# One PSUM tile of three banks becomes three tiles, and one copy of 1024 columns becomes two of 512

## The chip, the cores and the metric

The kernel runs on one core of a Trainium2 chip. The core has a tensor engine (PE), a vector engine (DVE), a scalar engine (ACT), GpSimd (POOL) and a sync engine (SP); here SP and POOL only issue DMAs once the start is over. The metric is the device time of one execution in microseconds (us). Lower is better.

## The reference

```python
def _attn_ref(q, k, v, tau):
    qn = q / (np.linalg.norm(q, axis=1, keepdims=True) + 1e-06)
    kn = k / (np.linalg.norm(k, axis=1, keepdims=True) + 1e-06)
    s = kn.transpose(0, 2, 1) @ qn / tau
    s = s - s.max(-1, keepdims=True)
    a = np.exp(s)
    a /= a.sum(-1, keepdims=True) + 1e-09
    return v @ a
...
def _moe_ref(x, w_in, w_out):
    h = x @ w_in
    g = h * (1.0 / (1.0 + np.exp(-h)))
    return g @ w_out
```

q, k and v are 2 x 6016 x 256 in float32. Attention is over the 256 channels, so each batch has one 256 x 256 matrix `a`. Its output, 12032 tokens of 256, goes through a feed-forward net of 2048 hidden channels: `w_in` (256 x 2048), SiLU, `w_out` (2048 x 256).

## The kernel before, in words

The kernel never forms `v @ a`. It multiplies `a` into `w_in` first (`mix`) and runs V, transposed, through the mixed weights. All large products run in float16, each operand as a high and a low half, three matmuls for each product (low x high, high x low, high x high). The first layer's 2 x 2 block products are computed with 7 block products in place of 8 (a Strassen-like scheme): sums of weight blocks S1 to S4 and of V blocks T1 to T4 are made ahead, and seven products are accumulated into three PSUM banks called z, y and x.

Tokens are worked in 12 pairs of up to 1024 columns, 6 to a batch; the last pair of a batch has 896. Pairs 0 and 5 are built by `emit_pair_group`, whose instructions a scheduler orders by priority and readiness. The other ten pairs are built by `emit_unit`, 8 units to a pair, and there PE, DVE and ACT keep the order in which the code is written. A unit works on two weight groups of 128 channels and on half of the pair's columns (256, or 224 in the last pair), so that a product is 6 matmuls of 256 columns that fill one bank of 512.

A unit goes like this. The products y (S1, L737) and x (A11, L738) are made, then one ACT copy moves both banks into `c51` (L740, 1024 columns). The product z (A12, L741) follows. `tail(0)` runs what earlier units left for this place. DVE subtracts z from the copied x (L743, helper L720). The products y (S4) and x (S2) are added into the banks (L745, L746), ACT copies x into `c2` (L748), DVE subtracts y from it (L751). The product x (S3, L753) follows, DVE subtracts the copied y from x (L754), the product x (A22, L758) follows. ACT applies SiLU to the four blocks (L723) and casts the top pair of them to float16 halves (L729, "high"); DVE makes the remainders (L732, "rest").

The second layer is spread over the next units. `out_of_unit` puts work into `later` lists: the remainder of the top pair, a sum of blocks that POOL makes by two DMAs (L902, L903, the second adding) and the cast of the low pair run in the next unit's `tail(0)`; the remainder of the low pair and a DVE sum (L896) in `tail(1)`; further sums, two of them by POOL's DMAs (L914, L915), in `tail(2)`. The second layer's matmuls (L822) are queued in groups of 4 and let out in blocks after each part of a unit: 8 matmuls after z, 12 after x (S2), 16 after x (S3), 8 after x (A22). After every fourth unit ACT copies four output banks (`take`, L866) and DVE joins them (L881, L885). In the gaps between the parts stand steps of background work: casts of the next pair's V (`scale_v`, ACT L164 and DVE L165), square sums of the transposed q and k in pairs 1 to 3, mixing for batch 1 in pairs 4 to 6.

The tile framework makes the semaphore waits. It follows every tile's readers and writers, so which tile a bank belongs to decides which waits it puts in.

Of the kernel before, what the change touches and what calls it, by code (L numbers as in the profile page):

```python
# [9 lines left out]
F32 = mybir.dt.float32  # L10
# [8 lines left out]
P = 128  # L19
# [11 lines left out]
def channel_attention_then_silu_ffn(ctx, tc, kq, qT, kT, vT, tau, w_in, w_out, outT):  # L31
    nc = tc.nc
# [12 lines left out]
    hp = ctx.enter_context(tc.tile_pool(name="hp", bufs=1))  # L45
    sm = ctx.enter_context(tc.tile_pool(name="sm", bufs=2))
    ps_b = ctx.enter_context(tc.tile_pool(name="ps_b", bufs=1, space=PSUM))
    zyx = ps_b.tile([P, 3, 512], F32, tag="zyx", name="zyx")
    z, y, x = (zyx[:, i] for i in range(3))
    ps_o = ctx.enter_context(tc.tile_pool(name="ps_o", bufs=4, space=PSUM))  # L50

    ident = const.tile([P, P], F32, name="ident")
# [29 lines left out]
    def room(name, n=1):  # L82

        k = turns[name] + turns[name] % n
        size = rooms[name].shape[1]
        k %= size
        turns[name] = (k + n) % size
        return rooms[name][:, k] if n == 1 else rooms[name][:, k : k + n]
# [611 lines left out]
    def emit_unit(p, u):  # L700


        b, n, w = pairs[p]
        h = w // 2
        m, alpha, sg = parts[p]
        which = 2 * (u % 4), 2 * (u % 4) + 1
        wide = h // 2
        at = u // 4 * wide

        def product(bank, a, x, first=False):  # L710
            for k, i in enumerate(which):
                for j, (v, c) in enumerate(((1, 0), (0, 1), (0, 0))):
                    nc.tensor.matmul(  # L713
                        bank[:, k * wide : (k + 1) * wide], mixed[b, i][:, v, a - 1],
                        m[:, c, x, at : at + wide], start=(first and j + k == 0),
                        stop=(j == 2), skip_group_check=True,
                    )

        def minus(g, a, c):
            nc.vector.tensor_tensor(out=g, in0=a[:, :h], in1=c[:, :h], op=ALU.subtract)  # L720

        def silu(src, g):
            nc.scalar.activation(out=g, in_=src, func=AF.Silu, scale=alpha)  # L723

        top, low = room("g", 2)[:, :, :h], room("g", 2)[:, :, :h]
        tops, lows = room("hl", 2)[:, :, :, :h], room("hl", 2)[:, :, :, :h]

        def high(hl, g):
            nc.scalar.activation(out=hl[:, :, 0], in_=g, func=AF.Copy, scale=sg)  # L729

        def rest(hl, g):
            nc.vector.scalar_tensor_tensor(  # L732
                out=hl[:, :, 1], in0=g, scalar=sg, in1=hl[:, :, 0], op0=ALU.mult,
                op1=ALU.subtract,
            )

        product(y, S1, T1, True)  # L737
        product(x, A11, B11, True)  # L738
        c51 = hp.tile([P, 2, 512], F32, tag="c51", name="c51")
        nc.scalar.copy(c51[:, :, :h], zyx[:, 1:, :h])  # L740
        product(z, A12, B21, True)  # L741
        tail(0)
        minus(top[:, 0], c51[:, 1], z)  # L743
        yield
        product(y, S4, B22)  # L745
        product(x, S2, T2)  # L746
        c2 = hp.tile([P, 512], F32, tag="c2", name="c2")
        nc.scalar.copy(c2[:, :h], x[:, :h])  # L748
        silu(top[:, 0], top[:, 0])
        tail(1)  # L750
        minus(top[:, 1], c2, y)  # L751
        yield
        product(x, S3, T3)  # L753
        minus(low[:, 1], x, c51[:, 0])  # L754
        silu(top[:, 1], top[:, 1])
        tail(2)
        yield
        product(x, A22, T4)  # L758
        silu(low[:, 1], low[:, 1])
        silu(x[:, :h], low[:, 0])  # L760
        high(tops, top)
        tail(3)
        out_of_unit(
            p, u, [tops[:, 0], tops[:, 1], lows[:, 0], lows[:, 1]], lambda: rest(tops, top),
            lambda: high(lows, low), lambda: rest(lows, low),
        )
        yield
# [4 lines left out]
    def tail(slot):  # L772

        for run in tails.pop(ticks[0], ()):
            run()
        ticks[0] += 1
# [555 lines left out]
```

## Time and profile before

| | |
|---|---|
| time, three runs | 1235.13, 1236.08 (median), 1240.56 us |
| the profiled execution | 1235.12 us, its span 1233.4 us |
| PE busy | 1065.3 us, 86% |
| DVE busy | 837.3 us, 68% |
| ACT busy | 815.0 us, 66% |
| POOL busy | 213.4 us, 17% |
| mean clock granted to PE | 0.988 of full speed |

The busy time of an engine is the time in which the profiler shows an instruction on it. Matmuls are pipelined and their ends are modelled, so consecutive matmuls overlap in the rows. An idle time is put down to the instruction that ended it, by semaphore events. The span is the profiled time of the program; the execution's own time is 1.7 us longer.

### The profile page before, as it was taken

The numbers are of one execution on the slowest core, as the hardware profiler recorded it, in microseconds if no ns is written. First come the engines' busy times: TensorE is split into PE (matmuls) and PEld (weight loads), VectorE is DVE, ScalarE is ACT, GpSimd is POOL, SyncE is SP. The second block draws the span as 40 slices with busy tenths as digits, with TensorE's granted clock in tenths as the row PEclk, the third lists the DMA queues.
The fourth block names the chain that finished last, engine by engine and source line by source line (L and its number), as shares of the span: only waits on it lengthen the run. The fifth ranks groups of instructions, "written<-read, shape, count | busy, mean of one in ns | idle before, by whom it ended". The sixth has DMA issues, their size and how long they took to land. (4 is left out here: it accounts for less than half of the span.)

```text
span 1233.4 us, 20497 instructions
## 1 busy us (share of the span) xinstructions
PE 1065.3 (86%) x8222; PEld 840.0 (68%) x8222; DVE 837.3 (68%) x1358; ACT 815.0 (66%) x1161; POOL 213.4 (17%) x301
## 2 busy tenths in 40 slices
PE   9999987887887887888999888888888888888886
PEld 8865534776766776766655677777777777777886
DVE  6895574675775666767778667767767767767665
ACT  6686666667675766666778566666666666666664
POOL 1010000211212121212100112212212212122232
PEclk9999998999998999999999999999999999999999
DMA  9982102544535535334200335335335335334444
GB/s 374 396 295 94 35 1 94 128 143 113 164 94 174 154 78 156 87 78 128 61 1 23 89 74 139 94 76 142 91 77 144 89 77 141 87 77 112 96 91 83
DMA packets 63793, 143.35 MB, mean 116 GB/s; under 512 B 6930, under 2 KB 21218, under 8 KB 63698
## 3 DMA queue, kind: packets, MB, share of 16 engines
q0 software_dynamic: 32944, 72.57, 25.3%
q1 hardware_dynamic: 30466, 68.95, 15.9%
q8 instruction: 64, 1.05, 0.4%
q10 hardware_dynamic: 288, 0.52, 0.1%
q14 instruction: 31, 0.25, 0.1%
HBM read 57.67 MB, written 12.32 MB: 57 GB/s over the span
## 5 line engine op out<-in xcount | busy, mean ns | idle before, releaser
L713 PE MATMUL zyx<-m,wall 128*128 128x256 f16 (+1 forms) x3360 | 433.0, 273 | 143.6 <-ACT c L740 92.1
L713 PEld LDWEIGHTS <-wall 128*128 128x128 f16 x3360 | 329.0, 98 | 228.9 <-issue 183.3
L732 DVE SCALAR_TENSOR_TENSOR hl<-g,sg,hl 128x1024 f16<-128x1024 f32 (+1 forms) x160 | 202.6, 1266 | 80.3 <-ACT hl L729 80.2
L822 PE MATMUL o<-hl,wo 128*128 128x256 f16 (+1 forms) x1920 | 240.9, 271 | 1.2 <-DVE hl L732 1.2
L822 PEld LDWEIGHTS <-wo 128*128 128x128 f16 x2240 | 218.9, 98 | 27.0 <-issue 2.2
L723 ACT ACTIVATE g<-g,alpha 128x512 f32<-128x512 f32 (+1 forms) x240 | 171.4, 715 | 53.9 <-DVE g L720 50.9
L729 ACT ACTIVATE hl<-g,sg 128x1024 f16<-128x1024 f32 (+1 forms) x160 | 181.4, 1134 | 0.0
L748 ACT COPY c<-zyx 128x512 f32<-128x512 f32 (+1 forms) x80 | 46.4, 580 | 175.6 <-PE zyx L713 172.4
L720 DVE TENSOR_TENSOR g<-c,zyx 128x512 f32<-128x512 f32 (+1 forms) x160 | 108.4, 678 | 62.2 <-PE zyx L713 47.5
L902 POOL DMA_DIRECT2D sums<-hl x79 | 49.3, 624 | 396.5 <-issue 170.7
L903 POOL DMA_DIRECT2D sums<-hl x79 | 70.2, 889 | 229.9 <-DMA sums<-hl 174.7
L720 DVE TENSOR_TENSOR g<-zyx,c 128x512 f32<-128x512 f32 (+1 forms) x80 | 54.8, 685 | 69.2 <-PE zyx L713 69.1
L621 PE MATMUL o<-hl,wo 128*128 128x512 f16 (+1 forms) x384 | 93.2, 372 | 3.1 <-ACT hl L164 1.9
L740 ACT COPY c<-zyx 128x1024 f32<-128x1024 f32 (+1 forms) x80 | 80.0, 1000 | 22.0 <-PE zyx L713 22.0
L723 ACT ACTIVATE g<-zyx,alpha 128x512 f32<-128x512 f32 (+1 forms) x80 | 54.4, 680 | 58.2 <-PE zyx L713 58.2
L652 PE MATMUL zyx<-m,wall 128*128 128x512 f16 (+1 forms) x336 | 84.7, 368 | 8.7 <-DVE g L663 6.3
L915 POOL DMA_DIRECT2D sums<-hl x60 | 53.7, 895 | 169.3 <-DMA sums<-t 61.5
L822 PE MATMUL o<-t,ws_lo 128*128 128x256 f16 (+1 forms) x320 | 74.6, 271 | 0.0
L822 PE MATMUL o<-t,ws_hi 128*128 128x256 f16 (+1 forms) x320 | 74.6, 271 | 0.0
L294 PE MATMUL sc<-kq_t 128*128 128x256 f32 x320 | 74.2, 380 | 0.4 <-DMA kq_t<-in_kq 0.4
L165 DVE SCALAR_TENSOR_TENSOR m<-v_t,sv,m 128x512 f16<-128x512 f32 (+2 forms) x46 | 34.8, 760 | 54.9 <-ACT m L164 54.9
L822 PEld LDWEIGHTS <-ws_hi 128*128 128x128 f16 x640 | 62.7, 98 | 10.7 <-issue 3.9
(180 smaller groups left out, 1372.6 us busy)
## 6 DMA issues: line engine op xcount, KB each, us to landing
sums<-hl POOLq DMA_DIRECT2D x198, 256.0 KB, 3.3
kq_t<-in_kq SPq DMA_DIRECT2D x39, 512.0 KB, 9.0
sums<-t POOLq DMA_DIRECT2D x54, 256.0 KB, 2.3
v_t<-in_vT SPq DMA_DIRECT2D x10, 1024.0 KB, 5.1
outT<-sb SPq DMA_DIRECT2D x40, 256.0 KB, 2.3
turned<-in_qT SPq DMA_DIRECT2D x10, 512.0 KB, 6.0
turned<-in_kT SPq DMA_DIRECT2D x10, 512.0 KB, 7.1
sums<-hl POOLq DMA_DIRECT2D x20, 224.0 KB, 3.7
```

The costliest lines, as they stand in the source:

```text
L294: nc.tensor.matmul(sc[:, cb, :], t[:, i, 0, cb * P : (cb + 1) * P], t[:, i, 1, :], start=(j + i == 0 and cb == 0), stop=(j + i == J - 1), ...
L621: nc.tensor.matmul(o[:, :h], a[:, f, ee], hl[:, m, :h], start=(c == 1 and i == 0), stop=(c == NF and i == 2),)
L652: nc.tensor.matmul(bank[:, :h], wm[:, u, a - 1], m[:, y, x, :h], start=(first and j == 0), stop=(j == 2), skip_group_check=True,)
L713: nc.tensor.matmul(bank[:, k * wide : (k + 1) * wide], mixed[b, i][:, v, a - 1], m[:, c, x, at : at + wide], start=(first and j + k == 0), ...
L720: nc.vector.tensor_tensor(out=g, in0=a[:, :h], in1=c[:, :h], op=ALU.subtract)
L723: nc.scalar.activation(out=g, in_=src, func=AF.Silu, scale=alpha)
L729: nc.scalar.activation(out=hl[:, :, 0], in_=g, func=AF.Copy, scale=sg)
L732: nc.vector.scalar_tensor_tensor(out=hl[:, :, 1], in0=g, scalar=sg, in1=hl[:, :, 0], op0=ALU.mult, op1=ALU.subtract,)
L740: nc.scalar.copy(c51[:, :, :h], zyx[:, 1:, :h])
L822: nc.tensor.matmul(o[:, side * wide : (side + 1) * wide], a, x, start=(first and j == 0), stop=(last and j == len(these) - 1), skip_group_ ...
L903: nc.gpsimd.dma_start(t1, b12, accum_op=ALU.add)
L915: nc.gpsimd.dma_start(t4, b21, accum_op=ALU.add)
```

## The change

The one tile `zyx` of three banks becomes three tiles z, y and x of a bank each, and the copy of two banks at once becomes a copy of y after the product y (S1) and a copy of x after the product x (A11). The size, the place and the arithmetic of everything else stay.

```diff
@@ -45,8 +45,7 @@
     ps_b = ctx.enter_context(tc.tile_pool(name="ps_b", bufs=1, space=PSUM))
-    zyx = ps_b.tile([P, 3, 512], F32, tag="zyx", name="zyx")
-    z, y, x = (zyx[:, i] for i in range(3))
+    z, y, x = (ps_b.tile([P, 512], F32, tag=k, name=k) for k in "zyx")
     ps_o = ctx.enter_context(tc.tile_pool(name="ps_o", bufs=4, space=PSUM))
@@ -735,9 +734,10 @@
         product(y, S1, T1, True)
+        c51 = hp.tile([P, 2, 512], F32, tag="c51", name="c51")
+        nc.scalar.copy(c51[:, 0, :h], y[:, :h])
         product(x, A11, B11, True)
-        c51 = hp.tile([P, 2, 512], F32, tag="c51", name="c51")
-        nc.scalar.copy(c51[:, :, :h], zyx[:, 1:, :h])
+        nc.scalar.copy(c51[:, 1, :h], x[:, :h])
         product(z, A12, B21, True)
```

In the changed kernel the lines from the tile on to the first product of a unit have numbers one lower: L713, L720, L723, L729 and L732 are L712, L719, L722, L728 and L731 there.

On PE, in the first unit of pair 8 (weight loads and matmuls alternate there; shown is each matmul that waits for a semaphore, and the first of some products and blocks where it waits for none). Before, the products in these rows are y (S1), z (A12) and y (S4); x (A11) and x (S2) wait for nothing and are left out:

```order
L713 MATMUL zyx<-m,wall 128x256 [waits Activation_49]
...
L713 MATMUL zyx<-m,wall 128x256 [waits Activation_49]
...
L822 MATMUL o<-sums,ws_lo 128x256 [waits DMASW4_49]
...
L822 MATMUL o<-sums,wo 128x256 [waits DMASW2_49]
...
L713 MATMUL zyx<-m,wall 128x256 [waits DVE_49]
...
L822 MATMUL o<-hl,wo 128x256
...
L822 MATMUL o<-hl,wo 128x256 [waits Activation_49]
...
L822 MATMUL o<-hl,wo 128x256 [waits DVE_49]
```

and now they are y (S1), x (A11), z (A12), y (S4) and x (S2):

```order
L712 MATMUL y<-m,wall 128x256
...
L712 MATMUL x<-m,wall 128x256 [waits Activation_49]
...
L712 MATMUL z<-m,wall 128x256
...
L822 MATMUL o<-sums,ws_lo 128x256 [waits DMASW4_49]
...
L822 MATMUL o<-sums,wo 128x256 [waits DMASW2_49]
...
L712 MATMUL y<-m,wall 128x256 [waits Activation_49]
...
L712 MATMUL x<-m,wall 128x256 [waits Activation_49]
...
L822 MATMUL o<-hl,wo 128x256 [waits DVE_49]
...
L822 MATMUL o<-hl,wo 128x256 [waits Activation_49]
...
L822 MATMUL o<-hl,wo 128x256 [waits DVE_49]
```

The order of the matmuls is the same. The waits moved: the first matmul of z had one for ACT and has none, that of y (S1) had one for ACT and it now stands at x (A11), and y (S4) waits for ACT where it waited for DVE. In the block of 12 over `hl` the second matmul has got a wait for DVE of its own, which the wait of y (S4) covered before; the waits of its second group, for ACT and then for DVE, stand as they did.

On ACT, in the same unit, from the cast of the top pair of the unit before to the copy `c2` (L748). Before:

```order
L723 ACTIVATE g<-zyx,alpha 128x512 [waits PE_49]
L729 ACTIVATE hl<-g,sg 128x2x512 [waits DMASW6_49,Activation_49]
L740 COPY c_8044<-zyx 128x1024 [waits PE_49]
L729 ACTIVATE hl<-g,sg 128x2x512 [waits DMASW7_49,DMASW0_49,Activation_49]
L748 COPY c_8077<-zyx 128x512 [waits DVE_49,PE_49]
L723 ACTIVATE g<-g,alpha 128x512
```

and now:

```order
L722 ACTIVATE g<-x,alpha 128x512 [waits PE_49]
L728 ACTIVATE hl<-g,sg 128x2x512 [waits DMASW6_49,Activation_49]
L738 COPY c_8088<-y 128x512 [waits PE_49]
L740 COPY c_8088<-x 128x512 [waits PE_49]
L728 ACTIVATE hl<-g,sg 128x2x512 [waits DMASW7_49,DMASW0_49,Activation_49]
L748 COPY c_8128<-x 128x512 [waits PE_49]
L722 ACTIVATE g<-g,alpha 128x512 [waits DVE_49] x2
```

One copy became two in the same place between the two casts, and `c2` no longer waits for DVE.

On PE, in pair 0, which the scheduler orders (`sc` are score products of batch 1, `w` is the mixing of a weight group; of each product one matmul is shown). Before:

```order
L652 MATMUL zyx<-m,wall 128x512
L294 MATMUL sc<-kq_t 128x256 x4
...
L652 MATMUL zyx<-m,wall 128x512
...
L294 MATMUL sc<-kq_t 128x256 x2
L434 LDWEIGHTS aT
L434 MATMUL w<-wi,aT 128x256
...
L652 MATMUL zyx<-m,wall 128x512
```

and now:

```order
L651 MATMUL y<-m,wall 128x512
...
L651 MATMUL x<-m,wall 128x512
...
L651 MATMUL z<-m,wall 128x512
...
L293 MATMUL sc<-kq_t 128x256 x3
...
L651 MATMUL y<-m,wall 128x512
...
L433 MATMUL w<-wi,aT 128x256
```

The three products of a unit now stand together, and score products and mixing that stood between them come behind.

## Rows read from the trace of the kernel before

**Rows 1.** The page, part 1: busy us (share of the span) and instructions.
```profile
PE 1065.3 (86%) x8222; PEld 840.0 (68%) x8222; DVE 837.3 (68%) x1358; ACT 815.0 (66%) x1161; POOL 213.4 (17%) x301
```

**Rows 2.** Waits: engine, line, what it waited for; us in all, times, longest.
```profile
PE zyx L713 <- ACT c L740: 92.1, 80, 1.7
...
PE zyx L713 <- DVE g L720: 26.8, 67, 0.8
...
PE zyx L713 <- ACT g L723: 14.7, 8, 4.6
```

**Rows 3.** Timeline, pair 8's first unit: start us, us, engine, line, operation [idle before].
```profile
864.71 1.01 ACT L740 COPY c<-zyx 128x1024 f32<-128x1024 f32 x1 [0.52 <-PE zyx L713]
...
865.77 0.81 PE L713 MATMUL zyx<-m,wall 128*128 128x256 f16 x6 [1.10 <-ACT c L740]
...
866.69 0.69 DVE L720 TENSOR_TENSOR g<-c,zyx 128x512 f32<-128x512 f32 x1 [1.19 <-PE zyx L713]
...
867.30 1.28 DVE L732 SCALAR_TENSOR_TENSOR hl<-g,sg,hl 128x1024 f16<-128x1024 f32 x1
...
867.43 1.47 PE L713 MATMUL zyx<-m,wall 128*128 128x256 f16 x12
...
868.74 1.47 PE L822 MATMUL o<-hl,wo 128*128 128x256 f16 x12
...
868.94 0.58 ACT L748 COPY c<-zyx 128x512 f32<-128x512 f32 x1 [2.17 <-PE zyx L713]
...
870.30 0.81 PE L713 MATMUL zyx<-m,wall 128*128 128x256 f16 x6
...
872.70 0.82 PE L713 MATMUL zyx<-m,wall 128*128 128x256 f16 x6
...
873.55 0.69 ACT L723 ACTIVATE g<-zyx,alpha 128x512 f32<-128x512 f32 x1 [0.89 <-PE zyx L713]
...
874.14 1.14 ACT L729 ACTIVATE hl<-g,sg 128x1024 f16<-128x1024 f32 x1
...
874.29 1.47 PE L713 MATMUL zyx<-m,wall 128*128 128x256 f16 x12
...
956.98 1.01 ACT L740 COPY c<-zyx 128x1024 f32<-128x1024 f32 x1 [0.52 <-PE zyx L713]
```

**Rows 4.** Timeline, that unit's end, and DVE behind the second unit.
```profile
875.18 0.68 ACT L866 ACTIVATE sb<-o,back 128x512 f32<-128x512 f32 x1
...
882.49 0.69 DVE L720 TENSOR_TENSOR g<-zyx,c 128x512 f32<-128x512 f32 x1 [0.91 <-PE zyx L713]
...
884.30 1.85 DVE L881 TENSOR_TENSOR sb<-sb 128x256 f32<-128x256 f32 x4
...
890.33 1.28 DVE L732 SCALAR_TENSOR_TENSOR hl<-g,sg,hl 128x1024 f16<-128x1024 f32 x1
```

**Rows 5.** The page, part 5: busy us, mean ns | idle before, what ended it.
```profile
L165 DVE SCALAR_TENSOR_TENSOR m<-v_t,sv,m 128x512 f16<-128x512 f32 (+2 forms) x46 | 34.8, 760 | 54.9 <-ACT m L164 54.9
```

**Rows 6.** Timeline of the last pair: the copies of its last two units.
```profile
1200.78 0.91 ACT L740 COPY c<-zyx 128x896 f32<-128x896 f32 x1 [0.47 <-PE zyx L713]
...
1210.75 0.91 ACT L740 COPY c<-zyx 128x896 f32<-128x896 f32 x1 [0.47 <-PE zyx L713]
```

**Rows 7.** Timeline at the border of pairs 1 and 2.
```profile
281.61 2.71 PE L713 MATMUL zyx<-m,wall 128*128 128x256 f16 x12 [4.61 <-ACT g L723]
```

**Rows 8.** Windows (pairs 0, 5): us, busy of each engine, PEclk, DMA share, GB/s.
```profile
61.00:191.00 130.00, 118.43 (x562) 67.34 (x561) 90.97 (x165) 93.78 (x149) 6.65 (x12) 0.98 0.29 103
...
580.00:674.00 94.00, 92.11 (x553) 53.35 (x551) 72.49 (x141) 70.84 (x120) 5.09 (x7) 1.00 0.11 26
```

**Rows 9.** Timeline: two issues of POOL in the unit of rows 3.
```profile
865.80 0.55 POOL L902 DMA_DIRECT2D sums<-hl  x1 [0.21 <-issue]
...
869.14 0.86 POOL L903 DMA_DIRECT2D sums<-hl  x1 [2.79 <-DMA sums<-hl]
```

**Rows 10.** The page, part 6: DMAs issued, KB each, median us to landing.
```profile
sums<-hl POOLq DMA_DIRECT2D x198, 256.0 KB, 3.3
```

## The prediction

> **What bounds the kernel now.** I read the busy shares first: TensorE (PE) 86%, VectorE (DVE) 68%, ScalarE (ACT) 66% [rows 1]. PE is the only candidate for a bound, so the question is what fills its other 14%, some 168 us. The view of waits answers it: PE's products into the three banks wait 80 times for the copy at L740, 92.1 us in all, once per unit; 67 times for the subtractions of L720, 26.8 us; 8 times for the SiLU of L723, 14.7 us [rows 2]. Then I read one unit in the timeline [rows 3]. It starts with the products y (S1) and x (A11); the copy of both starts when x ends and takes 1.01 us (864.71), and the product z begins 0.05 us after its end (865.77). z writes a bank that this copy doesn't read, so that wait is one of the tile and not of the data. The products y (S4) and x (S2) start at 867.43, 0.05 us after the subtraction of 866.69 ended, which reads z: the same kind. Each such wait costs 0.16 us more than its idle time, since a matmul's modelled end lies that far behind the start of what could follow it.
>
> What would PE need alone? Twelve matmuls go by in 1.31 us (867.43 to 868.74), 0.109 us each. A unit has 7 products of 6 and 44 matmuls of the second layer in blocks of 8, 12, 16 and 8: 86 x 0.109 = 9.37 us. A pair of 8 units took 956.98 - 864.71 = 92.27 us, 11.53 a unit [rows 3]. So 2.16 us a unit is the most that can go.
>
> **The change part by part.** Three tiles in place of one: by the order of PE, the first matmul of z now waits for nothing, that of y (S1) for nothing, y (S4) only for its own copy, x (S3) for the copy c2 alone and not for the subtraction that reads y. The true waits stay: x (A11) for the SiLU that reads x in the unit before, x (S2) for the copy of x, x (A22) for the subtraction that reads x.
>
> The copies: 1.01 us goes, two of 0.58 come (a copy of 512 columns is in [rows 3], 868.94): +0.15 us a unit on ACT, 12 us over 80 units. ACT is idle a third of the time, and nothing on PE waits for the second copy before x (S2), so I cost the split at nothing by itself. The Trainium skill speaks against it: "Advanced Engine Details and Errata", The Read-Write Bubble, says that ScalarE pays a latency between instructions, so large tiles are better, and that one instruction may read several banks. The row agrees in sign (1.16 against 1.01). By that rule alone the change would cost 12 us.
>
> What is late next? I walk one unit through with the durations of [rows 3], from t = 0 at the first product. The products and blocks of PE run: y 0, x 0.65, z 1.31, block of 8 at 1.96, y (S4) 2.83, x (S2) 3.49, block of 12 at 4.14, x (S3) 5.45, block of 16 at 6.10, x (A22) 7.85, block of 8 at 8.50, end 9.37. The SiLU of x starts 0.85 after x (A22) (872.70, 873.55), the scaled cast of the top pair 0.59 later (874.14), and ACT is free 1.04 after that (875.18 in [rows 4]): t = 0.96 of the next unit. The copy of y runs from 0.96, that of x from 1.54, the cast of the low pair from about 2.1 to 3.2, and DVE's remainder of the low pair (L732, 1.28 us) ends at about 4.5. The second matmul of the second group of the block of 12 reads that remainder and is due at 4.14 + 0.55 = 4.69. So a bare unit closes at 9.37 with some 0.2 us to spare: the loop over ACT and DVE is about as long as PE's own work. Everything else that stands ahead of that remainder is then paid by PE. Three kinds do:
> - Output copies (L866, 0.68 us, [rows 4]) and casts of the scaled V between the cast of the top pair and that of the low pair. Two L866 stand so in the second unit of each half pair: about 1.2 us, less the 0.2 to spare and 0.44 because a group more stands ahead in that unit: 0.5.
> - A long run on DVE behind the last subtraction of the second unit of each half: t2, the joins L881, L885, reductions, both remainders. It lasts from 882.49 to 890.33 + 1.28, 9.12 us, without a gap [rows 4]. In the new unit that subtraction starts at 6.3, with the 0.5 at 6.84; 6.84 + 9.12 - 9.87 = 6.09 in the next unit against 4.69 due: 1.4 to 1.5.
> - The remainder of the scaled V (L165, 0.76 us) ahead of DVE's remainder of the top pair, which itself waits for ACT; 54.9 us of DVE's idle time lies before it now [rows 5]. ACT casts at 0.96 to 1.67; then 0.75, 1.28, 0.6, 0.6 and 1.28 on DVE end at 6.2: 1.5.
>
> For the eight units of a pair I get 0, 0.5, 1.5, 0.5 (the small matmul into z waits for its reader), 1.5, 1.7, 2.1 and 0.4 us of new PE waits: 8.2 us. These are hand sums good to some 4 us a pair. From below such a wait is nothing, if the extras fall into gaps; from above it is the whole 17.3 us (8 x 2.16) that goes, so that the pair stays at 92.
>
> **Sum.** Nine full pairs: 92.27 - 74.96 - 8.2 = 9.1 us each, 82 us. The last pair (448 columns) takes 9.97 us a unit now [rows 6] and 9.37 x 224/256 = 8.2 by PE alone, without scaled V: 8 x 1.77 = 14, less 2 for its L866: 12 us. Three units at the borders of pairs hold long waits for ACT (4.61 us at 281.61 [rows 7]), whose cause is not the tile; I take 2 us each off the gain: -6. In the two pairs that a scheduler orders (0 and 5), the products of y, x and z of one unit move together and those of scores behind them, which the order shows for the first; PE is busy 118.43 of 130 us and 92.11 of 94 there [rows 8], so there is little to win; bounds 8 us faster and 8 slower (the 11.6 us idle of the first, nearly all), I take 0. The DMAs that POOL issues for the sums, and SP's queue, keep their order. Sum: -88 us. The profiled execution took 1235.1 us, 1.7 more than its span and 1.0 less than the median shown: 1235.1 - 88 = 1147.
>
> **Rivals.** A (forecast): the false waits go and ACT's and DVE's lateness takes half of it back: 1147, own range 1120 to 1172.
> B: all waits on the banks go and nothing takes their place; PE runs at 9.37. 72 x 2.16 + 14 - 6 = 164: 1071. For it: the sums of busy time on ACT and DVE leave room; the order of their work could hide every extra. Against it: the walk above; made with the old waits in place it gives 11 to 11.4 us a unit, close to the mean of 11.53.
> C: the sums that POOL makes by DMA come late. L903 is issued 3.34 us after L902 (865.80, 869.14) and lands 3.3 us later [rows 9, 10]; its reader is the block of 8 in the next unit, now at about 865.77 + 11.53 + 0.65 = 877.9, so 5 us are to spare. In the new unit: L902 at 2.4, L903 at 5.75, landed at 9.05, due at 11.3: 2.2 to spare. With more bytes per us in flight and both landings 1.5 us later, PE waits about 0.8 a unit for it, 64 us, of which I take 0.6 as not hidden in the other waits: +38: 1185.
> D (slower): the same chain sets the pace. Per unit POOL goes through L902, its landing, L903, then two more issues of which the second waits for a landing as well, in order: about 2 x (3.34 + 0.86) = 8.4 us. From the point where a landing takes 4.9 us and not 3.3, this is over 11.6 and each unit is longer than now; at 12.0 it costs 80 x 0.47 = 38: 1273. Against it: at the present pace POOL is busy 17% of the span [rows 1].
> E (no change): ACT's and DVE's order sets the pace already, and PE's wait only moves from z to the block of 12: 92 us a pair, 1235. Against it: the old unit's walk has slack on both engines right behind each false wait.
>
> **How the numbers follow.** A 0.60, B 0.15, C 0.17, D 0.04, E 0.04. The range runs from 1095 (between A's edge and B, since a gap in my hand sums is more likely than all of B) to 1190, past C: what lies outside is most of B, D and E, some 2 in 10. A measurement of this kernel can tell 0.5%, 6 us, from no change: faster 0.92 (A, B, C), same 0.04 (E), slower 0.04 (D).
>
> **What would show it.** Right: no wait of a product for the first copies except x (S2)'s; z starting 0.65 us after x; unit times near 9.4 in the first unit of a pair and 10 to 11.5 in the second, third and fifth to seventh; a new wait of PE's second layer for DVE's L731 (before: L732), some 60 to 80 us in all. Wrong: that wait near zero (B), or PE's second layer waiting for the DMA of the sums more than 20 us (C), or unit times still near 11.5 (E).

## The result

| | before | after |
|---|---|---|
| time, median | 1236.38 us (1235.13 to 1240.56, 4 runs) | 1139.28 us (1136.42 to 1141.50, 4 runs) |
| the profiled execution, its span | 1235.12, 1233.4 us | 1141.50, 1139.7 us |
| its mean granted clock of PE | 0.988 | 0.980 |

The ratio is 0.921 with a 95% interval of 0.917 to 0.924: 97 us faster. The forecast was 1147 (1095 to 1190). The busy shares of the changed kernel, from part 1 of its page, answer to [rows 1]:

```profile
PE 1034.9 (91%) x8222; PEld 847.2 (74%) x8222; DVE 830.2 (73%) x1358; ACT 812.4 (71%) x1241; POOL 213.9 (19%) x301
```

The work is the same, with 80 ACT instructions more. The waits of PE answer to [rows 2] (engine, line, what it waited for; us in all, times, longest):

```profile
PE o L822 <- DVE hl L731: 64.3, 61, 2.3
PE o L822 <- DMA sums<-hl: 17.9, 8, 4.9
PE x L712 <- ACT g L722: 9.9, 5, 3.7
```

The 92.1 us behind the copies and the 26.8 us behind the subtractions are gone. In their place stands mainly one new wait: the second layer waits for the remainder that DVE makes of the low pair (L731). Its wait for the DMA of the sums grew too, from 3.4 to 17.9 us. The first unit of pair 8 in the timeline answers to [rows 3] (start, us, engine, line, operation, idle before):

```profile
788.68 0.82 PE L712 MATMUL y<-m,wall 128*128 128x256 f16 x6
789.34 0.82 PE L712 MATMUL x<-m,wall 128*128 128x256 f16 x6
789.64 0.57 ACT L738 COPY c<-y 128x512 f32<-128x512 f32 x1
...
789.99 0.82 PE L712 MATMUL z<-m,wall 128*128 128x256 f16 x6
...
802.32 1.28 DVE L731 SCALAR_TENSOR_TENSOR hl<-g,sg,hl 128x1024 f16<-128x1024 f32 x1 [0.34 <-ACT hl L728]
...
803.66 0.49 PE L822 MATMUL o<-hl,wo 128*128 128x256 f16 x3 [0.30 <-DVE hl L731]
...
875.24 0.57 ACT L738 COPY c<-y 128x512 f32<-128x512 f32 x1
```

z starts 0.65 us after x (789.34, 789.99), beside the copy of y; before, 1.10 us of idle time lay ahead of it. The Trainium skill, "PSUM — Partial Sum Buffer", PSUM bank collisions raise a hardware error, says that engines have to be kept apart within a bank and a group of 32 partitions; it asks nothing of other banks, and this overlap agrees. The wait of 0.30 us at 803.66 ends 0.06 us after the remainder of 802.32, in the second unit: the new limit in one row. From copy to copy the pair takes 875.24 - 789.64 = 85.6 us; 92.27 before, 83.2 forecast.

Where the 93.7 us between the spans come from, by the starts of the product y (S1) in both timelines:

| stretch | before | after | change | forecast |
|---|---|---|---|---|
| start and pair 0 | 191.60 | 177.78 | -13.8 | 0 (±8, with pair 5) |
| pairs 1 to 4, without the last unit | 387.5 | 351.0 | -36.5 | -30 |
| that unit and pair 5 | 96.62 | 90.60 | -6.0 | 0 |
| pairs 6 to 10 | 463.66 | 423.45 | -40.2 | -45.5 |
| last pair and end | 93.97 | 96.89 | +2.9 | -12 |

### The profile page after: what moved, and what is told of

It reads as the page before. It is cut to its first block, busy times and chain, and to the rows that moved or that the text cites. A ratio compares the mean times of both kernels' runs of the same rounds, so it can differ in the third digit from the quotient of the medians.

```text
span 1139.7 us, 20504 instructions
## 1 busy us (share of the span) xinstructions
PE 1034.9 (91%) x8222; PEld 847.2 (74%) x8222; DVE 830.2 (73%) x1358; ACT 812.4 (71%) x1241; POOL 213.9 (19%) x301
## 5 line engine op out<-in xcount | busy, mean ns | idle before, releaser
L712 PEld LDWEIGHTS <-wall 128*128 128x128 f16 x3360 | 331.7, 99 | 52.8 <-issue 13.2
L822 PE MATMUL o<-hl,wo 128*128 128x256 f16 (+1 forms) x1920 | 254.3, 274 | 64.3 <-DVE hl L731 64.3
L822 PEld LDWEIGHTS <-wo 128*128 128x128 f16 x2240 | 222.1, 99 | 102.1 <-issue 75.0
L712 PE MATMUL x<-m,wall 128*128 128x256 f16 (+1 forms) x1920 | 263.5, 274 | 10.2 <-ACT g L722 9.9
L731 DVE SCALAR_TENSOR_TENSOR hl<-g,sg,hl 128x1024 f16<-128x1024 f32 (+1 forms) x160 | 202.7, 1267 | 87.7 <-ACT hl L728 87.0
L722 ACT ACTIVATE g<-g,alpha 128x512 f32<-128x512 f32 (+1 forms) x240 | 171.1, 717 | 92.5 <-DVE g L719 91.9
L728 ACT ACTIVATE hl<-g,sg 128x1024 f16<-128x1024 f32 (+1 forms) x160 | 182.0, 1138 | 0.0
L712 PE MATMUL y<-m,wall 128*128 128x256 f16 (+1 forms) x960 | 132.7, 275 | 0.1
L902 POOL DMA_DIRECT2D sums<-hl x79 | 49.7, 629 | 351.4 <-DVE hl L731 107.6
L903 POOL DMA_DIRECT2D sums<-hl x79 | 70.2, 889 | 221.3 <-DMA sums<-hl 158.1
L748 ACT COPY c<-x 128x512 f32<-128x512 f32 (+1 forms) x80 | 46.6, 583 | 76.3 <-PE x L712 75.0
L722 ACT ACTIVATE g<-x,alpha 128x512 f32<-128x512 f32 (+1 forms) x80 | 54.3, 679 | 51.9 <-PE x L712 51.9
L620 PE MATMUL o<-hl,wo 128*128 128x512 f16 (+1 forms) x384 | 87.2, 366 | 0.1
L915 POOL DMA_DIRECT2D sums<-hl x60 | 53.7, 896 | 174.6 <-ACT c L738 52.8
L719 DVE TENSOR_TENSOR g<-x,c 128x512 f32<-128x512 f32 (+1 forms) x80 | 54.6, 683 | 29.8 <-PE x L712 29.8
L164 DVE SCALAR_TENSOR_TENSOR m<-v_t,sv,m 128x512 f16<-128x512 f32 (+2 forms) x46 | 34.8, 761 | 55.1 <-ACT m L163 54.9
L822 PEld LDWEIGHTS <-ws_lo 128*128 128x128 f16 x640 | 63.6, 99 | 7.5
L293 PEld LDWEIGHTS sc<-kq_t 128*128 128x128 f32 x320 | 60.0, 190 | 10.9 <-DMA kq_t<-in_kq 1.6
```

Source lines behind the costliest of these rows:

```text
L293: nc.tensor.matmul(sc[:, cb, :], t[:, i, 0, cb * P : (cb + 1) * P], t[:, i, 1, :], start=(j + i == 0 and cb == 0), stop=(j + i == J - 1), ...
L620: nc.tensor.matmul(o[:, :h], a[:, f, ee], hl[:, m, :h], start=(c == 1 and i == 0), stop=(c == NF and i == 2),)
L712: nc.tensor.matmul(bank[:, k * wide : (k + 1) * wide], mixed[b, i][:, v, a - 1], m[:, c, x, at : at + wide], start=(first and j + k == 0), ...
L731: nc.vector.scalar_tensor_tensor(out=hl[:, :, 1], in0=g, scalar=sg, in1=hl[:, :, 0], op0=ALU.mult, op1=ALU.subtract,)
L822: nc.tensor.matmul(o[:, side * wide : (side + 1) * wide], a, x, start=(first and j == 0), stop=(last and j == len(these) - 1), skip_group_ ...
L902: nc.gpsimd.dma_start(t1, b11)
```

## The experiments

Each was timed beside the kernel before; ratios are to that kernel. "A pair" is the time of pair 8, and a unit's time runs from the start of its product y (S1) to that of the next one.

**The copies alone.** One tile as before, two copies:

```diff
         product(y, S1, T1, True)
...
+        nc.scalar.copy(c51[:, 0, :h], y[:, :h])
         product(x, A11, B11, True)
...
-        nc.scalar.copy(c51[:, :, :h], zyx[:, 1:, :h])
+        nc.scalar.copy(c51[:, 1, :h], x[:, :h])
```

> One tile of three banks as before, but the copy made as two of 512 columns, each behind its own product. Theory (the waits come from the tile, not from the data): the product x (A11) now has to wait for the copy of y, and z for the copy of x. Walked from the start of the unit: ACT free at 0.96, copy of y to 1.54, x at 1.59, copy of x 2.45 to 3.03, z at 3.08 where it stood at 2.57 before: +0.5 us a unit, 80 units: 1265 to 1285 us. Rival (the gain of the change comes from the earlier, shorter copies): 1140 to 1180 us. Rival (the copies' form is without effect): 1236.

Measured: 1311.1 us, ratio 1.061 (1.058 to 1.063). The direction is the theory's, the size is past it. Its waits of PE:

```profile
PE zyx L713 <- ACT c L739: 86.4, 80, 1.9
PE zyx L713 <- ACT c L741: 53.4, 80, 0.7
```

With one tile the product x now waits for the copy of y as well, and z for that of x: 139.8 us behind copies in place of 92.1. This run differs from the changed kernel in the tile alone, and it is 172 us slower: that is what the tile is worth with two copies. On ACT the two copies are busy 45.5 + 46.5 us and the one 80.0 (80 times 569, 581 and 1000 ns): the split costs 12 us of ACT, as the prediction had it. The rule that the prediction drew on (the Trainium skill, "Advanced Engine Details and Errata", The Read-Write Bubble) accounts for those 12 us and no more. Much of what goes past the theory can be clock. The profiled executions, before and here:

```profile
core 0: 1233.4 us, clock 0.988
...
core 0: 1310.2 us, clock 0.965
```

Of full speed, 0.012 of 1233.4 us (15 us) was not granted before, and 0.035 of 1310.2 us (46 us) here. So up to 31 of the 75 us are clock (an estimate, and an upper bound, since PE is not the limit all the time). The 44 left are 0.55 us a unit, where the theory had 0.5. A smaller copy was of use here only once nobody waited for the other banks of its tile.

**z alone.** z gets a tile, y and x share one and its copy of 1024 columns:

```diff
-    zyx = ps_b.tile([P, 3, 512], F32, tag="zyx", name="zyx")
-    z, y, x = (zyx[:, i] for i in range(3))
+    z = ps_b.tile([P, 512], F32, tag="z", name="z")
+    yx = ps_b.tile([P, 2, 512], F32, tag="yx", name="yx")
+    y, x = (yx[:, i] for i in range(2))
...
-        nc.scalar.copy(c51[:, :, :h], zyx[:, 1:, :h])
+        nc.scalar.copy(c51[:, :, :h], yx[:, :, :h])
```

> z is a tile of its own, y and x share one tile of two banks, with the one copy of 1024 columns as before. Theory (every false wait counts, and what ACT does ahead of the cast of the low pair is paid by PE): z waits for nothing, but x (S3) waits again for the subtraction that reads y, y (S1) for the SiLU that reads x, and the copy starts only when x ends, 0.3 us later for the cast behind it. About 0.5 to 0.6 us a unit more than the changed kernel: 1180 to 1195 us. Rival (only z's wait mattered): 1137 to 1150 us.

Measured: 1187.2 us, ratio 0.960 (0.959 to 0.962): the theory. Half of the change's gain, 49 us, is z's. The other 48 come with the tiles of y and x and the earlier copy of y, which weren't separated. Most of it stands in one wait here: the product x (S3) waits for the subtraction that reads y, since y and x still share a tile (L714, 36.1 us):

```profile
PE o L823 <- DVE hl L733: 58.0, 57, 1.9
PE yx L714 <- DVE g L721: 36.1, 76, 0.8
```

A pair takes 89.5 us. The new wait for the remainder is there already, with 58.0 us: it follows from a faster unit, not from the second copy.

**The remainder's readers last.** In the changed kernel, two of the groups of matmuls that read no low-pair remainder are queued ahead of those that do:

```diff
             add("a", 0, cross(1, 0, b11), False),
+            add("d", 0, high(1, b11, b21), False),
+            add("d", 1, high(1, b12, b22), end),
             add("c", 0, cross(0, 0, b21), False),
...
-            add("d", 0, high(1, b11, b21), False),
-            add("d", 1, high(1, b12, b22), end),
```

> The changed kernel, with the groups of the second layer let out in another order: in the block of 12 the two groups that read only high halves of the low pair stand ahead, and the group that reads DVE's remainder of the low pair comes at the head of the block of 16, 1.4 us later. Theory (the new waits of the second layer for L731, 64.3 us over 61 times, are lateness of under 1.5 us and cost PE in full): that wait falls to 10 to 20 us and the time to 1080 to 1100 us. Rival (the loop over ACT and DVE sets the pace, so the wait only moves to the next group or to x (A22)): 1125 to 1140 us with other waits of 50 us or more.

Measured: 1108.9 us, ratio 0.897 (0.895 to 0.900), 30 us less than the changed kernel. Its waits of PE:

```profile
PE o L822 <- DMA sums<-hl: 25.3, 16, 4.9
PE x L712 <- ACT g L722: 19.6, 13, 5.0
PE o L822 <- DVE hl L731: 9.5, 23, 0.8
PE x L712 <- DVE g L719: 4.5, 7, 1.3
```

The wait fell from 64.3 to 9.5 us, but 7.4, 9.7 and 4.5 us came back in the three others: of 55 us of that wait, 22 turned up elsewhere. The result lies between the two expectations, nearer to the theory: DVE's lateness was real, and two fifths of it stood in front of the next lateness.

**The last pair's sums without POOL.** In the changed kernel, the sums t1 and t4 of the last pair are made by DVE and not by POOL's DMAs:

```diff
         def first_sum():
-            if last:
+            if p == len(pairs) - 1:
...
-            if end:
+            if end or p == len(pairs) - 1:
```

> The changed kernel, with the sums t1 and t4 of the last pair made by DVE in place of POOL's two DMAs each. Theory (in the last pair PE waits for the DMA of the sums, 12.7 us over 5 times, because its units are shorter and its landings longer): these waits go, DVE has room (43.5 of 68.8 us busy), and the time falls by 10 to 14 us: 1125 to 1130 us. Rival (DVE's run behind every second unit takes the place of the DMA): 1136 to 1142 us, with waits for L731 or L896 in the last pair.

Measured: 1130.0 us, ratio 0.915 (0.912 to 0.918): the theory, at the upper end of its range. The runs (1126.15 to 1134.52 us) all lie below those of the changed kernel (1136.42 to 1141.50). Seven units of the last pair take 62.6 us, against 68.8 in the changed kernel. PE's wait for the DMA of the sums falls from 17.9 us to

```profile
PE o L822 <- DMA sums<-hl: 6.6, 4, 3.2
```

The rival holds in a small part. In those seven units the wait for L731 is now

```profile
PE o L822 <- DVE hl L731: 3.2, 6, 1.2
```

where it was 0.3 us in the changed kernel.

**Both.** The last two edits together.

> The changed kernel with both: the second layer's matmuls over the remainder come last in their unit, and the last pair's sums t1 and t4 are made by DVE and not by POOL's DMAs. Theory: two separate costs, PE's wait for DVE's remainder (54.8 us fewer in e3_late_rest, which gave 30 us) and the DMA of the sums in the last pair (9 us in e4_last_dve). e3 had taken 3.5 us of the last pair already (68.8 to 65.3 us for seven units), so 1139 - 30 - 9 + 3 = 1103: 1097 to 1107. Rival: in the last pair the two additions make DVE late for the remainder again and nothing more is won than by the order alone: 1108 to 1114.

Measured: 1095.1 us, ratio 0.885 (0.881 to 0.889): 2 us under the theory's range. The gains alone, 30.4 and 9.3, add to 39.7, and 44.1 came: the two costs are separate, and the 4 us more are within the intervals. Its waits:

```profile
PE x L712 <- ACT g L722: 19.3, 11, 5.0
PE o L822 <- DMA sums<-hl: 12.0, 16, 1.8
PE o L822 <- DVE hl L731: 11.2, 27, 0.9
```

**V's casts a gap earlier.** In the changed kernel, the ACT casts and DVE remainders of the next pair's V stand in the first three of a unit's four gaps, in place of the first, third and fourth (only in the pairs of `emit_unit`):

```diff
-                    p == 0 or slot in ((0, 2, 3) if p in paired else ...
+                    p == 0 or slot in ((0, 1, 2) if p in paired else ...
```

> The changed kernel with the casts of the next pair's V in the first, second and third of the four gaps of a unit in place of the first, third and fourth (pairs 1 to 3, 5 and 8 as the source lists them excepted where another rule stands; only the pairs that scale V in three gaps change). Theory: the ACT cast and DVE remainder of V that stand in the fourth gap delay the casts of the next unit and so DVE's remainder of the low pair; PE's wait for L731 falls by 20 us or more: 1115 to 1125. Rival: a gap earlier they delay other work by as much: 1135 to 1145, L731's wait 55 to 75.

Measured: 1108.9 us, ratio 0.896 (0.892 to 0.899). The theory's sign, but 6 us better than its range. The wait for L731 fell as expected, by 26.6 us:

```profile
PE o L822 <- DVE hl L731: 37.7, 43, 2.3
```

In pair 8 the fifth to seventh units take 9.51, 9.84 and 11.00 us, against 10.78, 10.92 and 13.33: these are the units in which V's remainder stood ahead of the low pair's (L164 in the changed kernel, 34.8 us in all). Part of the rest is clock (below): the 13.33 held 1.7 us of it, and the mean granted clock of the four runs, 0.988 against 0.983, makes up to 6 us of the whole (an estimate: 0.0115 of 1109 us not granted here, 0.0168 of 1139 there).

**All three edits.**

> e5_both with the casts of V moved as in e6_v_slots. Theory: the move acts through PE's wait for DVE's remainder alone, which the late order has already taken away, so nothing is added: within 5 us of e5_both, 1095 to 1107. Rival: it acts on waits that the late order leaves (products waiting for ACT's SiLU, 19.6 us, and the DMA of sums, 25.3 us) as well, and adds 10 us or more: 1080 to 1093.

Measured: 1091.9 us, ratio 0.882 (0.878 to 0.885), 3 us under both edits without the third. By the difference that is the theory (within 5 us, where the rival asked for 10 or more); by the time alone it lies in the rival's range, because the run with both edits came out lower than expected. The intervals overlap, so these two can't be told apart. Moving V's casts and moving the remainder's readers are two cures of one lateness: 30 us each alone, no more than 3 on top of each other. The wait for L731 fell from 11.2 to 3.3 us, and that of the products for L719 rose from 4.7 to 13.3. Its waits show the next limit, spread over three releasers:

```profile
PE x L712 <- ACT g L722: 21.2, 9, 5.0
PE o L822 <- DMA sums<-hl: 14.6, 14, 3.5
PE x L712 <- DVE g L719: 13.3, 25, 1.4
```

This is the fastest version run, 144 us under the kernel before.

## Why the prediction came out right, step by step

**The false waits.** Held. The bank waits at L740 and L720 are gone, and the two parts of the edit were told apart as far as they can be: the second copy brings time only with the tiles (-49 us for z's tile alone, +75 us for the copies alone, -97 us for all of it). Three tiles with both copies in the old place, behind the product x, were not run, so what the earlier copy of y adds is open.

**What is late next.** Held, in place and in size: a wait of PE's second layer for L731 of 60 to 80 us was forecast, 64.3 came. That it costs time was shown by two ways of removing it, 30 us each. The unit times of pair 8, by the starts of y (S1), less the 9.37 us of PE's own work:

| unit | 0 | 1 | 2 | 3 | 4 | 5 | 6 | 7 | sum |
|---|---|---|---|---|---|---|---|---|---|
| forecast | 0 | 0.5 | 1.5 | 0.5 | 1.5 | 1.7 | 2.1 | 0.4 | 8.2 |
| measured | 0.0 | 0.5 | 1.3 | 0.3 | 1.4 | 1.6 | 4.0 | 1.6 | 10.6 |

The first six are within 0.3 us of the walk. The seventh unit takes 11.66 us in pairs 6 and 7, 2.3 over, and 13.33 in pair 8, where the clock fell. The eighth is the one that the walk missed, by 1.2 us: there too PE waits for L731. Rival B, by which nothing would take the waits' place, is 68 us too fast.

**Pairs 0 and 5.** The term was mis-sized: 0 with bounds of ±8, measured -13.8 and -6.0, together -19.8. Its step was "PE is busy 118.43 of 130 us and 92.11 of 94 there, so there is little to win". The windows of the same two stretches in the changed kernel answer to [rows 8] (us, busy of each engine and instructions, PEclk, DMA share, GB/s):

```profile
61.00:177.78 116.78, 113.51 (x562) 66.86 (x561) 90.28 (x164) 91.86 (x148) 6.74 (x12) 1.00 0.31 115
...
528.78:619.38 90.60, 89.48 (x566) 54.99 (x564) 72.50 (x143) 70.94 (x123) 5.11 (x7) 1.00 0.11 27
```

The 562 matmuls of pair 0 that were busy for 118.43 us are now busy for 113.51: 4.9 us lay inside busy time, beside 8.3 us of idle time (11.57 to 3.27). Part of the 4.9 is clock: 0.98 was granted before and 1.00 now, which is at most 2.6 us in 130. In pair 5, with the last unit of pair 4, the clock is the same and busy time fell by 4.6 us (94.11 to 89.48), idle time by 1.4. The window before:

```profile
579.10:675.72 96.62, 94.11 (x564) 54.63 (x563) 74.21 (x144) 73.43 (x123) 5.09 (x7) 1.00 0.11 27
```

Where such time hides can be read in the timeline of before, in pair 5:

```profile
601.00 0.49 PE L822 MATMUL o<-sums,wo 128*128 128x256 f16 x3
601.49 0.73 PE L652 MATMUL zyx<-m,wall 128*128 128x448 f16 x3
```

Three matmuls at 0.109 us let the next begin at 601.33; it began at 601.49, and no idle time is shown, since the modelled end of the third covers the 0.16 us. Such gaps stand between alternating products all through the pair: by the starts of consecutive matmuls they come to some 5.8 us in that window before and to 1.4 in the changed kernel (an estimate). How much of the two gains is the waits and how much the new order of the scheduler wasn't separated; with z's tile alone pair 1 starts at 180.80 us, with the copies alone at 191.70.

**The last pair.** The term failed: -12 forecast, +2.9 measured (-1.2 in the first seven units, +4.1 behind them). The step took PE's own work (8.2 us a unit) as what is left, and rival C's arithmetic with the durations of pair 8 (issues of 0.55 and 0.86 us, a landing of 3.3). In the last pair POOL's issues read, in the changed kernel:

```profile
1068.86 1.20 POOL L903 DMA_DIRECT2D sums<-hl  x1 [2.87 <-DMA sums<-hl]
1069.61 1.20 POOL L914 DMA_DIRECT2D sums<-t  x1
1073.84 1.20 POOL L915 DMA_DIRECT2D sums<-hl  x1 [3.04 <-DVE t L896]
...
1078.68 1.20 POOL L903 DMA_DIRECT2D sums<-hl  x1 [2.89 <-DMA sums<-hl]
```

From L903 to L903 it is 9.82 us, 5.93 of them idle ahead of L915 and L903, the two DMAs that add to what the one before them wrote. (The first idle time is put down to DVE; L915 follows L914 as L903 follows L902.) The kernel before has the same round in its last pair:

```profile
1161.93 1.21 POOL L915 DMA_DIRECT2D sums<-hl  x1 [2.48 <-ACT c L740]
...
1171.71 1.20 POOL L915 DMA_DIRECT2D sums<-hl  x1 [2.54 <-DVE hl L732]
```

That is 9.78 us beside a unit of 9.97 [rows 6]: POOL's round took nearly the whole unit there already, and PE had no wait for it in those units, because the false waits made each unit just longer than the round. When they went, the wait for the DMAs came out:

```profile
1072.59 0.26 PE L822 MATMUL o<-sums,ws_lo 128*128 128x224 f16 x1 [1.93 <-DMA sums<-hl]
1082.39 0.26 PE L822 MATMUL o<-sums,ws_lo 128*128 128x224 f16 x1 [1.40 <-DMA sums<-hl]
1094.15 0.35 PE L822 MATMUL o<-sums,ws_lo 128*128 128x224 f16 x1 [3.36 <-DMA sums<-hl]
...
1095.60 1.32 PE L712 MATMUL y<-m,wall 128*128 128x224 f16 x6
...
1099.96 0.74 PE L712 MATMUL x<-m,wall 128*128 128x224 f16 x6
...
1114.65 0.26 PE L822 MATMUL o<-sums,ws_lo 128*128 128x224 f16 x1 [1.11 <-DMA sums<-hl]
...
1126.20 0.34 PE L822 MATMUL o<-sums,ws_lo 128*128 128x224 f16 x1 [4.87 <-DMA sums<-hl]
```

These five are 12.7 of the 17.9 us: rival C, true in one pair of twelve. The experiment on the last pair's sums confirms it (62.6 us for the seven units, without POOL). Why an issue takes 1.20 us there and 0.86 or 0.55 in pair 8 wasn't tried.

**The sum.** The errors have both signs: pairs 0 and 5 gave 20 us more than forecast, pairs 1 to 4 gave 6.5 more, pairs 6 to 10 gave 5.3 less, the last pair 15 less. The total was 6 us off between the spans, and much of that is luck. The sum also has no term for the clock. It shows in the first unit of pair 1 (before, then in the changed kernel):

```profile
191.60:206.98 15.38, 13.40 (x67) 7.64 (x67) 4.34 (x7) 7.29 (x12) 0.00 (x0) 0.75 0.12 44
...
177.78:187.76 9.98, 9.93 (x67) 6.45 (x66) 4.77 (x7) 7.04 (x13) 0.00 (x0) 1.00 0.08 28
```

The 0.25 not granted is at most 3.8 of the 5.4 us between them. In the units where the clock fell in the changed kernel (below), it took time away.

## What to carry to other kernels

Count the banks that one tile holds before splitting a copy: a dependency that is followed by tile makes the writer of one bank wait for the readers of all, and a smaller copy in a shared tile only added waits here. A wait that goes uncovers the next one in line, so walk one unit through with the new pace, for each kind of unit apart (the short last pair had another limit than the rest), with the durations of that stretch. Work of late readers goes behind work of early ones; look for that order before making the late engine faster.

## What the runs showed that was not expected

A wait of the same length can cost twice. In the changed kernel the seventh unit of pairs 7 and 8 has the same wait, and the matmuls behind it differ (pair 7, then pair 8; between them units are left out):

```profile
772.99 0.92 PE L822 MATMUL o<-hl,wo 128*128 128x256 f16 x7 [1.80 <-DVE hl L731]
...
856.92 1.14 PE L822 MATMUL o<-hl,wo 128*128 128x256 f16 x7 [1.80 <-DVE hl L731]
857.85 1.49 PE L712 MATMUL x<-m,wall 128*128 128x256 f16 x6
...
861.75 0.82 PE L712 MATMUL x<-m,wall 128*128 128x256 f16 x6
```

In pair 8 six matmuls take 1.49 us at first and 0.82 four us later. The windows around say why: the granted clock, the third figure from the end, is below full speed right behind the wait:

```profile
851.00:856.90 5.90, 3.96 (x35) 3.25 (x34) 5.87 (x9) 4.05 (x7) 1.42 (x2) 1.00 0.63 167
856.90:860.00 3.10, 3.08 (x18) 2.27 (x18) 1.91 (x4) 1.33 (x2) 0.86 (x1) 0.59 1.00 340
860.00:863.00 3.00, 3.00 (x25) 2.53 (x24) 1.33 (x3) 1.12 (x2) 0.56 (x1) 0.85 0.78 198
```

So the clock was at the lower of its two levels (1.2 of 2.4 GHz) for about 3.4 of those 6.1 us (a share of 0.41 of 3.10 us and 0.15 of 3.00 us, 1.7 us together, was not granted, and the lower level withholds half). The unit took 1.7 us longer (13.33 against 11.66). In the last pair the wait of 3.36 us at 1094.15 is followed by products of 1.32 us in place of 0.74, and the end after the wait of 4.87 us ran at 0.75. Short waits don't always leave the clock alone. In its last pair the kernel before had a wait of 1.0 us in each unit and a granted clock of 1.00 (1140 to 1210). Pair 10, before and with the copies alone:

```profile
1047.74:1139.38 91.64, 79.51 (x691) 67.18 (x690) 62.95 (x96) 59.39 (x80) 19.79 (x28) 1.00 0.38 93
...
1107.48:1210.19 102.71, 86.89 (x691) 70.54 (x690) 63.46 (x96) 60.05 (x88) 19.79 (x28) 0.93 0.34 83
```

The longest wait of PE in it is 1.6 us before and 1.8 with the copies alone, where each unit has two waits for copies in place of one, and the clock was granted for 0.93. What makes one wait cost the clock and another not was not tried.

The end of the changed kernel, from the last unit's start on, takes 28.05 us where it took 23.95. It holds the wait of 4.87 us (the longest there was 2.47 before) and the low clock behind it.
